# A mixture-of-experts tail that starts one step earlier: first products at step 48, the fourth weight split there, twice the routing from step 45, and the low halves of the second weights last

## The chip, the cores and the metric

The kernel runs on one core of one Trainium2 chip. The time is device microseconds of that core, the median of three runs. The profile is one further execution, with its own time.

## The reference, cut to what matters

Attention over short windows and block sums gives `x` (3072 tokens of 512). Every token then goes to one of 16 experts, chosen in two levels, and the expert's two products give its output row.

```python
g_idx = np.argmax(x @ w_group, axis=1)                   # 4 groups
e_idx = np.argmax(xg @ w_expert[g], axis=1)              # 4 experts in each
h  = np.maximum(xg[mask_e] @ w1[g, e], 0.0)              # 512 -> 1024
ye = h @ w2[g, e]                                        # 1024 -> 512
out[tok_idx] = (g_w * e_w)[mask][:, None] * ye
```

## The kernel before

Every engine has its own queue, and the order in each queue is the order in which the program writes its instructions; nothing is reordered by a scheduler.

**Attention** is a loop over `n` from 0 to 50. Sixteen pairs of heads have three groups of query tiles each, so 48 steps have scores, and steps 48 to 50 only drain the pipeline. A step writes the letters of `PLAN[n % 3]` in order: `s` scores, `e` exponentials, `t` transposes of the probabilities of step n-2, `v` the products with the values of step n-3, `l0` to `l3` the router logits of earlier pairs of heads (`l0` and `l1` transpose parts of `x`, `l2` multiplies them with the router weights, `l3` puts the logits in place), `p` and `b` the preparation of the next pair. At the end of each step `hook(n, ...)` writes a piece of the expert part.

**Routing** of a quarter of the tokens (768) is a generator, `Router.route`, of some thirty small VectorE operations and seven small TensorE products (the ranks). It is drawn forward by `advance(ops)` at places in `scores` and `values` (`OPS`: one operation after the scores, one after the reciprocal, one after the multiplication). The third quarter's routing is put on the list at step 40 behind `first_blocks`, which picks the fullest expert and the tokens of its first four blocks of 128. What is left of the list after the loop is written out at once. The fourth quarter's, with the tables of all later units, is `fin`; it can start only after attention.

**The first expert**, `Experts.first()`, is also a generator. Its weights are kept as two numbers each, a rounded high half (ScalarE copies it, `w1h`, `w2h`) and a low half (VectorE subtracts, `w1l`, `w2l`); so are its inputs (`xT`) and its hidden values (`hTh`, `hTl`). `split_w` makes one of four parts of either weight. `stage1_2` does the first products for 256 tokens in eight portions of 12 TensorE products (128 hidden columns each); here a portion is called a block, 0 to 7. After each second block the ReLU and its low half follow. The results lie in PSUM banks that are used in rotation, so block 6 needs the bank that the low half of blocks 2 and 3 frees. `stage2` does the second products for 128 tokens, 24 in four portions.

Step numbers that matter: `hook(47)` transposes the first 256 tokens (`x_t1`) and splits part 3 of the first weights; `FIRST` says how many portions of `first()` are written in `hook(49)`, `hook(50)` and `hook(51)`, the last of which stands behind the loop: two, one and one.

After attention, `first()` and `fin` are woven by a count of planned time: after each portion, operations of `fin` are drawn while the counted VectorE time is behind the counted TensorE time. Every VectorE operation of the expert part counts, the low halves of weights too. At the tag `units` everything left of `fin` is written, and the weights and tokens of the later experts' units follow.

```python
        for tag in first:
            ...
            while clock.dve < clock.pe and idle < 2:
                before = clock.dve
                next(fin, None)
```

Of the kernel before, what the change touches and what calls it, by code (L numbers as in the profile page):

```python
# [8 lines left out]
F32 = mybir.dt.float32  # L9
# [5 lines left out]
ALU = mybir.AluOpType  # L15
# [5 lines left out]
P = 128  # L21
# [25 lines left out]
KC, FC = DM // P, FF // P  # L47
# [13 lines left out]
OPS = dict(r=1, m=1, k=2, s=(1, 1, 1))  # L61


W1_AT = 34
GATHER_AT, W2_AT, X_AT = 4, 2, 1
SPLIT_AT = (-4, -3, -2, -1)
FIRST = {1: 2, 2: 1, 3: 1}

XT_AT = 4

# [4 lines left out]
class Banks:  # L75
# [5 lines left out]
    def next(self):  # L81
        self.n += 1
        return self.tiles[(self.n - 1) % len(self.tiles)]
# [6 lines left out]
class Clock:  # L90

    pe, dve = float("-inf"), 0.0
    step = 0


def columns(ap):
# [494 lines left out]
def attention(tc, q, k, v, w_group, w_expert, ident, x_dram, ps, router, hook):  # L591
# [3 lines left out]
    clock = router.clock  # L595

    def advance(ops):

        for _ in range(ops):
            r = next(work[0], work) if work else "wait"  # L600
            if r is work:
                work.pop(0)
            elif r == "wait":
                break
# [11 lines left out]
    with ExitStack() as st, ExitStack() as nat_st:  # L616
# [6 lines left out]
        order = [(b, a) for b in range(B) for a in range(NP)]  # L623
# [37 lines left out]
        t = ps_lg.next()  # L661
# [57 lines left out]
        def block_sums(idx):  # L719

            sp = ps_tr.next()[:, 0:2 * D]
            va = va_ring[idx % NVA]
            for i in range(NQT // 4):
                for j in range(4):
                    T.matmul(out=sp[32 * j:32 * j + 32], lhsT=pick[:, i], rhs=va[0:KW, NQT // 4 * j + i, :, 0:D],
                             start=(i == 0), stop=(i == NQT // 4 - 1), skip_group_check=True)
            vss[idx] = sm.tile([P, 2 * D], F32, name="vs", bufs=2)
            V.tensor_copy(out=vss[idx], in_=sp)
# [67 lines left out]
        def scores(n):  # L796

            idx, g = n // 3, n % 3
            qt, kw = qts[idx % 2], kws[idx % 2]
            sp = [ps_s.next()[:, 0:2 * NC].rearrange("p (j c) -> p j c", j=2) for _ in range(2)]  # L800
            for j in range(2):
                for i, h in ((0, 0), (1, 1), (1, 0), (0, 1)):
                    t, rows = 4 * g + 2 * j + i, slice(64 * h, 64 * h + 64)
                    T.matmul(out=sp[h][64 * i:64 * i + 64, j], lhsT=qt[rows, QT * t:QT * t + QT],
                             rhs=kw[rows, t], start=True, stop=True, skip_group_check=True)
            nm = sm.tile([P, 4], F32, name="nm")
            ss = sm.tile([P, 4, NC], F32, name="ss", bufs=2)
            for h in range(2):
                for j in range(2):
                    u, t = 2 * h + j, 4 * g + 2 * j  # L810
                    V.tensor_tensor_reduce(out=ss[:, u], in0=mask[:, 1 if t == 0 else 2 if t == NQT - 2 else 0],  # L811
                                           in1=sp[h][:, j], scale=1.0, scalar=3.4e38, op0=ALU.add, op1=ALU.min,
                                           accum_out=nm[:, u:u + 1])
            advance(OPS["s"][g])
            return ss, nm
# [90 lines left out]
        for n in range(NG + 3):  # L906
            idx, g = n // 3, n % 3
            if n < NG:
                b, a = order[idx]
                xs[b] = x_ring[b % 2]  # L910
            for step in PLAN[g]:
                if step == "s" and n < NG:
                    sps = scores(n)
                    if n == 0:
                        block_sums(0)
                        put_vs(0)
                        router.consts()
                elif step == "e" and n < NG:
                    prs[n] = exps(n, *sps)
                elif step == "t" and 0 <= n - T_LAG < NG:  # L920
                    pts[n - T_LAG] = transpose_p(prs.pop(n - T_LAG))
                elif step == "v" and 0 <= n - V_LAG < NG:
                    values((n - V_LAG) // 3, (n - V_LAG) % 3, pts.pop(n - V_LAG))
                elif step[0] == "p" and n < NG and idx + 1 < len(order):
                    prep(idx + 1, int(step[1]))
                elif step == "b" and n < NG and idx + 1 < len(order):
                    block_sums(idx + 1)
                elif step[0] == "l" and 0 <= idx - LAG[step] < len(order):
                    logits(idx - LAG[step], int(step[1]))
            if n == 0:  # L930
                init_va(2)
                spread_vs(0)
                init_va(3)
            if n in ROUTE_AT:
                b1 = ROUTE_AT.index(n)
                work.append(router.route(b1 * TB, (b1 + 1) * TB))
                if b1 == 1:
                    work.append(router.first_blocks())
            if n == NG - 4:
                nat_st.close()  # L940
            if n < NG:
                if g == 0 and 0 < idx < len(order) - 3:
                    qk[idx + 3] = load_qk(idx + 3)
                if g == 0 and idx + 2 < len(order):
                    load_vw(idx + 2)
                if g == 2 and idx + 1 < len(order):
                    put_vs(idx + 1)
                if g == 0 and idx > 0:
                    spread_vs(idx)
            if g == 1 and stores:  # L950
                store()
            while stores and n == NG - 5:
                store()
            clock.step += 1
            hook(n, need, w1_space)
        for part in (1, 2):
            logits(len(order) - 1, part)
# [9 lines left out]
class Experts:  # L967
# [79 lines left out]
            cs = slice(n * hh, n * hh + n)  # L1047
            queue.dma_start(out=dst[:, cs], in_=src[bass.ds(e, 1), :, cs].rearrange("a p c f -> (a p) c f"), **kw)

    def split_w(self, row, which, parts, copy=None, sub=None):  # L1050

        raw = self.raw(row, which)
        for c in parts:
            js = slice(2 * c, 2 * c + 2)
            if which == 0:
                src = raw.rearrange("p c (j r) -> p c j r", j=FC)[:, :, js]
                h, l = (t[:, :, js] for t in self.w1s)
            else:
                src = raw[:, js]
                h, l = (t[:, js] for t in self.w2s)  # L1060
            (copy or self.nc.scalar.copy)(out=h, in_=src)  # L1061
            (sub or self.V).tensor_tensor(out=l, in0=src, in1=h.bitcast(F32), op=ALU.subtract)

    def gather(self, row, dst, half=0):
        name, c = self.col(row, half)
# [13 lines left out]
        nc.scalar.copy(out=hi, in_=tp)  # L1079
        self.V.tensor_tensor(out=lo, in0=tp, in1=hi.bitcast(F32), op=ALU.subtract)  # L1080

    def stage2(self, hT, row, half=0, b=0):

        nc = self.nc
        yp = self.bank("av", b)
        wh, wl = self.w2s
        hi, lo = hT
        for c in range(FC):
            for i, (a, w) in enumerate(((hi, wh), (hi, wl), (lo, wh))):
                self.T.matmul(out=yp, lhsT=a[:, c], rhs=w[:, c], start=(c == 0 and i == 0),  # L1090
                                 stop=(c == FC - 1 and i == 2), skip_group_check=True)
            if c % 2 == 1:
                yield
        if not self.fixed:
            self.ny = (self.ny + 1) % 2
        y = self.y[b if self.fixed else self.ny]
        name, col = self.col(row, half)
        w = self.tabs[name, "weight"][:, col:col + 1]
        self.nc.scalar.activation(out=y, in_=yp, func=AF.Copy, scale=w)  # L1099
        self.put(y, row, half)  # L1100
# [160 lines left out]
    def first(self):  # L1261
        for i in range(0, NE, 2):
            for k, _ in enumerate(self.stage1_2(0)):
                if i == 0 and k >= 4:
                    self.split_w(("first", 0), 1, [k - 4])
                yield
            if i + 2 < NE:
                self.x_t1()
                yield
            for half in range(2):  # L1270
                s2 = self.stage2([t[:, :, half * P:half * P + P] for t in self.hT2], ("first", i + half))
                if i + half < NE - 1:
                    yield from s2
        yield "units"
        for part, _ in enumerate(s2):
            self.split_w(("unit", 0), 0, [part])
            if part == 0:
                self.x_t2(0)
                for i in range(2):
                    self.gather_one(i)  # L1280
                self.gather_small(0)
        self.fixed = True
# [51 lines left out]
def block_attention_then_moe(tc, q, k, v, w_group, w_expert, w1, w2, out):  # L1334
    with ExitStack() as st:
# [15 lines left out]
        def hook(n, need, space):  # L1351

            if not ex.w1r and n >= W1_AT and (router.ready & 1 or n == last - 4):
                need(1)
# [14 lines left out]
            for part in range(4):  # L1369
                if n == last + SPLIT_AT[part]:  # L1370
                    ex.split_w(("first", 0), 0, [part])
            for _ in range(FIRST.get(n - last, 0)):
                next(first)
# [63 lines left out]
```

## Time and profile before

| | |
|---|---|
| median of three runs | 547.08 us (546.47 to 547.29) |
| time of the profiled execution | 550.22 us |
| its span, first to last instruction | 548.4 us |
| TensorE matmul busy | 495.0 us, 90% |
| VectorE busy | 312.6 us, 57% |
| ScalarE busy | 289.4 us, 53% |
| GpSimd busy | 150.3 us, 27% |
| mean granted TensorE clock | 0.961 |

The busy shares are means over stages. Attention fills about the first 199 us of the span, the first expert's four blocks reach to about 257 us, and units of other experts, with weights loaded meanwhile, fill the rest.

### The profile page before, as it was taken

The page shows a single profiled execution, that of the slowest core. Times are in us where ns is not written, and L with a number is a line of the kernel's source. Part 1 is how long each engine was busy: PE and PEld are TensorE (multiplying, and loading weights), DVE is VectorE, ACT ScalarE, POOL GpSimd, SP SyncE. Part 2 cuts the span into 40 slices and gives each one's busy share as a digit, 9 for nine tenths or more (in the row PEclk, how much of TensorE's full clock was granted, in tenths as well). Part 3 has the DMA queues.
Part 4 walks back from the last instruction along what each step waited for, and adds up shares of the span by engine and source line. Part 5 has one row for each costly group of instructions (what it writes and reads, how often), then busy time and mean ns, then how long its engine had stood idle before and what let it go on. Part 6 is the DMA issues. An engine that isn't in the chain of part 4 may idle for free. (4 is left out here: it accounts for less than half of the span.)

```text
span 548.4 us, 13166 instructions
## 1 busy us (share of the span) xinstructions
PE 495.0 (90%) x4873; PEld 415.3 (76%) x4873; DVE 312.6 (57%) x1001; ACT 289.4 (53%) x561; POOL 150.3 (27%) x166
## 2 busy tenths in 40 slices
PE   6799888898988688999989999899999999999991
PEld 3577666676767577978959788788898998977770
DVE  6667788788876558856725436274564737540000
ACT  5678878899977423114715444364454735541110
POOL 6453453363444100035222040412120212201110
PEclk9789999999988799988998999999999999999997
DMA  9676785695671620099916969666667657746950
GB/s 211 151 179 133 182 194 141 160 219 145 144 272 40 232 77 16 24 331 388 384 51 265 393 222 395 232 237 247 218 231 250 208 179 228 258 118 214 322 195 22
DMA packets 80837, 111.15 MB, mean 203 GB/s; under 512 B 42732, under 2 KB 51310, under 8 KB 77936
## 3 DMA queue, kind: packets, MB, share of 16 engines
q1 hardware_dynamic: 74992, 93.31, 54.8%
q0 software_dynamic: 4704, 14.69, 7.2%
q10 hardware_dynamic: 1056, 2.10, 1.1%
q8 instruction: 44, 0.72, 0.6%
q14 instruction: 41, 0.34, 0.2%
HBM read 118.27 MB, written 13.04 MB: 239 GB/s over the span
## 5 line engine op out<-in xcount | busy, mean ns | idle before, releaser
L122 PE MATMUL ps_s<-xT,w1h 128*128 128x256 f32 x448 | 85.0, 287 | 1.9 <-DVE hTl L122 1.4
L122 DVE TENSOR_TENSOR w2l<-w2r,w2h 128x1024 fp32r<-128x1024 f32 x40 | 48.8, 1225 | 54.3 <-ACT w2h L1061 52.4
L1105 POOL DMA_INDIRECT out_dram<-y,t_unit_scatter x21 | 21.9, 1044 | 196.4 <-ACT y L1099 107.8
L122 PEld LDWEIGHTS ps_s<-xT,w1h 128*128 128x128 f32 x448 | 71.4, 193 | 3.3 <-DVE hTl L122 1.7
L122 PE MATMUL ps_s<-xT,w1l 128*128 128x256 f32 x224 | 63.7, 284 | 0.0
L820 ACT ACTIVATE pr<-ss,nm 128x120 f32<-128x120 f32 x192 | 60.1, 388 | 4.4 <-DVE nm L811 4.0
L1143 ACT ACTIVATE hTh<-ps_s 128x512 fp32r<-128x512 f32 x44 | 26.3, 598 | 53.1 <-PE ps_s L122 33.1
L749 POOL TENSOR_TENSOR va<-vr,share 24x512 f32<-24x512 f32 x48 | 49.7, 1060 | 12.5 <-DMA vr<-vs 8.9
L122 DVE TENSOR_TENSOR w1l<-w1r,w1h 128x1024 fp32r<-128x1024 f32 x40 | 46.4, 1221 | 2.9 <-ACT w1h L1061 2.7
L122 PE MATMUL ps_s<-ohr,w1h 128*128 128x256 f32 x256 | 47.8, 285 | 0.0
L122 DVE SCALAR_TENSOR_TENSOR hTl<-ps_s,hTh 128x512 fp32r<-128x512 f32 x44 | 30.4, 691 | 25.2 <-ACT hTh L1143 24.3
L811 DVE CUSTOM_DVE_ANT_0 ss<-mask,ps_s 128x120 f32<-128x120 f32 x192 | 41.9, 273 | 4.2 <-ACT pr L820 2.4
L1061 ACT CAST w2h<-w2r 128x1024 fp32r<-128x1024 f32 x40 | 41.5, 1042 | 4.3 <-DVE w_all L122 3.6
L122 PEld LDWEIGHTS ps_s<-xT,w1l 128*128 128x128 f32 x224 | 43.2, 193 | 0.2
L122 PEld LDWEIGHTS ps_s<-ohr,w1h 128*128 128x128 f32 x256 | 40.3, 190 | 0.7 <-issue 0.6
L828 ACT COPY ptS<-ps_tr 121x512 f32<-121x512 f32 x48 | 28.2, 587 | 20.9 <-PE ps_tr L122 9.4
L1061 ACT CAST w1h<-w1r 128x1024 fp32r<-128x1024 f32 x40 | 38.9, 1047 | 0.0
L789 POOL COPY kw<-kf 128x1152 f32<-128x1152 f32 x15 | 17.4, 1157 | 77.5 <-DVE kf L780 43.4
L776 ACT ACTIVATE qt<-ps_tr 64x384 f32<-64x384 f32 x64 | 33.3, 521 | 7.2 <-PE ps_tr L122 6.4
L122 PE MATMUL ps_s<-kw,qt 64*64 64x120 f32 x768 | 34.4, 287 | 2.9 <-DVE kw L756 2.1
L122 PE MATMUL ps_av<-va,ptS 121*64 121x65 f32 x768 | 34.3, 234 | 2.8 <-POOL va L749 1.4
L122 PE MATMUL ps_s<-ohr,w1l 128*128 128x256 f32 x128 | 36.2, 283 | 0.0
(255 smaller groups left out, 1055.7 us busy)
## 6 DMA issues: line engine op xcount, KB each, us to landing
w1r<-in_moe_w_dram SPq DMA_DIRECT2D x40, 1024.0 KB
w2r<-in_moe_w_dram SPq DMA_DIRECT2D x40, 1024.0 KB
va<-in_v_dram SPq DMA_DIRECT2D x32, 240.0 KB
kn<-in_k_dram SPq DMA_DIRECT2D x16, 384.0 KB
qn<-in_q_dram SPq DMA_DIRECT2D x16, 384.0 KB
x_dram<-xt SPq DMA_DIRECT2D x12, 512.0 KB
w_first<-in_moe_w_dram SPq DMA_DIRECT2D x2, 1024.0 KB
w2r<-in_moe_w_dram ACTq DMA_DIRECT2D x2, 1024.0 KB
```

Of the source, the lines that this page charges most:

```text
L122: return f(*args, **kw)
L749: nc.gpsimd.tensor_tensor(out=va_ring[idx % NVA][KW:NC, t:t + n, :, 0:D], in0=vr[KW:NC].broadcast_to([NBLK, n, 2, D]), in1=by(share, KW, N ...
L776: nc.scalar.activation(out=by_run(qb, h)[:, j], in_=tv, func=AF.Copy, scale=-1.0 / 8.0)
L789: (nc.gpsimd if idx else V).tensor_copy(out=kw[:, :, 0:KW], in_=tiles)
L811: V.tensor_tensor_reduce(out=ss[:, u], in0=mask[:, 1 if t == 0 else 2 if t == NQT - 2 else 0], in1=sp[h][:, j], scale=1.0, scalar=3.4e38, ...
L820: nc.scalar.activation(out=pr[:, i, 0:NC], in_=sp[:, i], func=AF.Exp, bias=nm[:, i:i + 1], scale=-1.0)
L828: nc.scalar.copy(out=ptS.rearrange("p a c -> p (a c)"), in_=pt[0:NR])
L1061: (copy or self.nc.scalar.copy)(out=h, in_=src)
L1105: self.nc.gpsimd.indirect_dma_start(out=out, out_offset=bass.IndirectOffsetOnAxis(ap=self.tabs[name, "scatter"][:, col:col + 1], axis=0), ...
L1143: nc.scalar.activation(out=th[:, js], in_=hp, func=AF.Relu)
```

## The change

Four things are edited. Part 3 of the first weights is split in `hook(48)` and not in `hook(47)` (`SPLIT_AT`). One portion of `first()` is written in each of `hook(48)` to `hook(51)`, where two, one and one stood in the last three (`FIRST`). From step 46 on, every `advance` draws twice as many routing operations (`MORE_AT`, `MORE`; the step number is noted only at the end of a step, so 45 takes effect in step 46). And the four low halves of the first expert's second weights leave the first products' portions: each is now written in front of a pair of columns of the first `stage2`, in which all products with low halves of weights stand behind the other sixteen.

```diff
+MORE_AT, MORE = 45, 2
-SPLIT_AT = (-4, -3, -2, -1)
-FIRST = {1: 2, 2: 1, 3: 1}
+SPLIT_AT = (-4, -3, -2, 0)
+FIRST = {0: 1, 1: 1, 2: 1, 3: 1}
@@ advance
-        for _ in range(ops):
+        for _ in range(ops * (MORE if clock.n >= MORE_AT else 1)):
@@ attention, end of a step
             clock.step += 1
+            clock.n = n
             hook(n, need, w1_space)
@@ split_w(self, row, which, parts, what="hl")
-            (copy or self.nc.scalar.copy)(out=h, in_=src)
-            (sub or self.V).tensor_tensor(out=l, in0=src, in1=h.bitcast(F32), op=ALU.subtract)
+            if "h" in what:
+                self.nc.scalar.copy(out=h, in_=src)
+            if "l" in what:
+                self.V.tensor_tensor(out=l, in0=src, in1=h.bitcast(F32), op=ALU.subtract)
@@ stage2(self, hT, row, half=0, b=0, late=None)
-        for c in range(FC):
-            for i, (a, w) in enumerate(((hi, wh), (hi, wl), (lo, wh))):
-                self.T.matmul(out=yp, lhsT=a[:, c], rhs=w[:, c], start=(c == 0 and i == 0),
-                                 stop=(c == FC - 1 and i == 2), skip_group_check=True)
-            if c % 2 == 1:
+        terms = (hi, wh), (hi, wl), (lo, wh)
+        if late:
+            order = [(c, t) for c in range(FC) for t in (0, 2)] + [(c, 1) for c in range(FC)]
+        else:
+            order = [(c, t) for c in range(FC) for t in range(3)]
+        for k, (c, t) in enumerate(order):
+            a, w = terms[t]
+            if late and t == 0 and c % 2 == 0:
+                late(c // 2)
+            self.T.matmul(out=yp, lhsT=a[:, c], rhs=w[:, c], start=(k == 0), stop=(k == len(order) - 1),
+                          skip_group_check=True)
+            if k % 6 == 5:
                 yield
@@ first
                 if i == 0 and k >= 4:
-                    self.split_w(("first", 0), 1, [k - 4])
+                    self.split_w(("first", 0), 1, [k - 4], what="h")
...
-                s2 = self.stage2([t[:, :, half * P:half * P + P] for t in self.hT2], ("first", i + half))
+                s2 = self.stage2([t[:, :, half * P:half * P + P] for t in self.hT2], ("first", i + half),
+                                 late=None if i + half else lambda c: self.split_w(("first", 0), 1, [c], what="l"))
```

## Rows read from the trace of the kernel before

**Rows 1.** Windows: length, busy us (instructions) of each engine, clock, DMA share, GB/s.

```profile
160.00:200.00 40.00, 33.52 (x388) 27.34 (x389) 20.04 (x87) 19.44 (x44) 11.35 (x10) 0.83 0.41 146
...
400.00:440.00 40.00, 40.00 (x268) 36.75 (x267) 26.82 (x28) 22.86 (x30) 7.16 (x7) 1.00 0.62 214
```

**Rows 2.** Waits of TensorE, 170 to 262 us: total us, times, longest.

```profile
PE ps_lg L122 <- DVE xT L865: 3.9, 3, 2.5
PE ps_tr L122 <- DVE eb L122: 1.7, 1, 1.7
PE ps_s L122 <- DVE hTl L122: 1.4, 1, 1.4
PE ps_av L122 <- DVE mx L122: 1.3, 1, 1.3
```

**Rows 3.** Windows of 4 us around step 48, columns as in rows 1.

```profile
184.00:188.00 4.00, 1.25 (x11) 0.42 (x11) 2.99 (x8) 1.38 (x2) 0.00 (x0) 0.66 0.84 322
188.00:192.00 4.00, 4.00 (x32) 3.64 (x29) 0.84 (x4) 0.59 (x1) 0.00 (x0) 0.50 0.29 108
192.00:196.00 4.00, 4.00 (x45) 3.76 (x44) 0.68 (x4) 1.28 (x3) 0.00 (x0) 0.98 0.33 126
```

**Rows 4.** Timeline of TensorE, steps 48 to the first second products: start, us, instruction.

```profile
183.23 0.69 PE L122 MATMUL ps_av<-va,ptS 121*64 121x65 f32 x16 [1.31 <-DVE mx L122]
...
187.18 0.87 PE L122 MATMUL ps_lg<-xT,wcat 128*32 128x192 f32 x8 [2.50 <-DVE xT L865]
...
190.19 0.58 PE L122 MATMUL ps_s<-xT,w1h 128*128 128x256 f32 x1
...
194.01 0.60 PE L122 MATMUL ps_tr<-ident,xt 128*128 128x128 f32 x4
...
195.16 0.38 PE L122 MATMUL ps_s<-xT,w1h 128*128 128x256 f32 x1
...
199.67 0.22 PE L122 MATMUL ps_tr<-eb,tri 128*128 128x96 bf16 x1
...
204.47 0.39 PE L122 MATMUL ps_s<-xT,w1h 128*128 128x256 f32 x1 [1.45 <-DVE hTl L122]
...
207.45 1.13 PE L122 MATMUL ps_tr<-ident,xg 128*128 128x128 f32 x8
208.34 0.47 PE L122 MATMUL ps_av<-w2h,hTh 128*128 128x512 f32 x1
```

**Rows 5.** Timeline of TensorE, the rest of the first pair's second products.

```profile
214.42 0.20 PE L122 MATMUL ps_tr<-eb,tri 128*128 128x96 bf16 x1 [1.65 <-DVE eb L122]
...
216.17 0.48 PE L122 MATMUL ps_s<-w2h,hTh 128*128 128x512 f32 x1
...
221.83 0.28 PE L122 MATMUL ps_s<-xT,w1h 128*128 128x256 f32 x1
```

**Rows 6.** Timeline of VectorE, step 47 to the fourth quarter's routing.

```profile
183.50 1.29 DVE L122 TENSOR_TENSOR xT<-ps_tr,xT 128x512 fp32r<-128x512 f32 x2 [0.22 <-ACT xT L1079]
184.92 1.23 DVE L122 TENSOR_TENSOR w1l<-w_first,w1h 128x1024 fp32r<-128x1024 f32 x1
...
186.71 0.42 DVE L865 COPY xT<-ps_tr 128x256 f32<-128x256 f32 x1
...
205.13 2.36 DVE L122 TENSOR_TENSOR w2l<-w2r,w2h 128x1024 fp32r<-128x1024 f32 x2 [0.71 <-ACT w2h L1061]
...
212.07 0.27 DVE L122 TENSOR_REDUCE mx<-lg 128x30 f32<-128x120 f32 x1
```

**Rows 7.** Timeline of ScalarE, the first high halves of second weights.

```profile
204.05 2.00 ACT L1061 CAST w2h<-w2r 128x1024 fp32r<-128x1024 f32 x2 [3.58 <-DVE w_all L122]
```

**Rows 8.** The page's groups: busy us, mean ns of one, idle before.

```profile
L1143 ACT ACTIVATE hTh<-ps_s 128x512 fp32r<-128x512 f32 x44 | 26.3, 598 | 53.1 <-PE ps_s L122 33.1
L122 DVE SCALAR_TENSOR_TENSOR hTl<-ps_s,hTh 128x512 fp32r<-128x512 f32 x44 | 30.4, 691 | 25.2 <-ACT hTh L1143 24.3
```

**Rows 9.** Timeline of the SP queue: the first loads of a unit's weights.

```profile
233.47 0.92 SPq L1048 DMA_DIRECT2D w1r<-in_moe_w_dram  x2
```

More of the change, by code (lines that the diff above doesn't have):

```diff
@@ L92 @@
     pe, dve = float("-inf"), 0.0
-    step = 0
+    step, n = 0, 0
 def columns(ap):
@@ L1048, in load_w, with split_w @@
             queue.dma_start(out=dst[:, cs], in_=src[bass.ds(e, 1), :, cs].rearrange("a p c f -> (a p) c f"), **kw)
-    def split_w(self, row, which, parts, copy=None, sub=None):
+    def split_w(self, row, which, parts, what="hl"):
         raw = self.raw(row, which)
@@ L1080, in split_t, with stage2 @@
         self.V.tensor_tensor(out=lo, in0=tp, in1=hi.bitcast(F32), op=ALU.subtract)
-    def stage2(self, hT, row, half=0, b=0):
+    def stage2(self, hT, row, half=0, b=0, late=None):
         nc = self.nc
```

## The prediction

> **What bounds the kernel now.** I read the windows first. In a later stage TensorE is busy for all of 40 us at full clock; from 160 to 200 us it is busy for 33.5 of 40 at a granted clock of 0.83, with VectorE at 20.0 and ScalarE at 19.4 [rows 1]. So TensorE sets the pace, and the turn from attention to the first expert is where it loses time, without another engine being full. The list of TensorE's waits says by whom: all the large ones end at VectorE [rows 2]. The timeline then places them: 1.31 us at 183.23 before the values of step 45, 2.50 at 187.18 before the logits `l2` of step 49, 1.45 at 204.47 before block 6 [rows 4], and 1.65 at 214.42 before the fourth quarter's rank products [rows 5]. [...] The two blocks that start at 190.19 need 3.82 us to 194.01, where the two from 204.47 to 207.45 need 2.98 [rows 4]. The change touches all but the first of these.
>
> **Step 47 to block 3.** VectorE's queue explains the 2.50 us. The low halves of `xT` run from 183.50 for 1.29, then the low half of weight part 3 from 184.92 for 1.23, and only behind it the copy at 186.71 (0.42) that `l2` waits for [rows 6]. With part 3 a step later that copy moves up by about a microsecond, and block 0 stands in TensorE's queue ahead of `l2`, so the wait is filled twice over. The split itself is moved, not removed: its subtraction now follows the copy, and nothing needs it before block 6; if that cover were gone it would cost its 1.23.
>
> Up to 183.23 I expect no change. The routing drawn in steps 46 and 47 is about ten operations instead of five. By the 0.27 of one such operation [rows 6] that is at most 1.35 us more on VectorE, spread over two steps in which the values wait 1.31 anyway [rows 4]; I take 0. In step 48 the doubled routing already writes the third quarter's rank products, and these take a transpose bank in the rotation of three. So `l1`'s transposes must now wait for the second low half of `xT`, to 183.50 + 1.29 = 184.79, and block 0 starts at about 185.2 (0.4 for two transposes; four start and yield to the next work within the 1.15 from 194.01 to 195.16 [rows 4]).
>
> Block 0 costs 1.49 at full clock (half of 2.98) and at most 2.98 at the lower level. The window around it showed 0.66, and TensorE has just had gaps, so I put it at the lower level, where the measured pair allows at least 3.82 - 1.49 = 2.33; I take 2.6, to 187.8. `l2`, the transposes and the values of step 49 took 3.01 (187.18 to 190.19) at the lower level; at full clock I estimate 1.5. With gaps gone the clock should rise in between: 2.0, to 189.8. Block 1 takes 1.49 (191.3). The next 1.15 (194.01 to 195.16) stays (192.45). From there to 199.67 it was 4.51 [rows 4]; I add 0.4, because about four routing operations (0.27 each) now stand on VectorE in front of the copy that the last `l2` waits for, and that wait was already part of the 3.9 [rows 2]. Block 3 ends at 197.4 instead of 199.67: **2.3 us gained**. Bounds: full clock throughout gives 185.2 + 1.49 + 1.5 + 1.49 + 1.15 + 4.9 = 195.8, a gain of 3.9; the lower level until 192, as before, leaves about 0.5.
>
> [...]
>
> **The rest of routing and block 6.** Before, the rest of the third quarter's routing is written behind block 3 and VectorE works on it up to 204 us. It keeps the low half of hidden values back, on whose bank block 6 waits 1.45 [rows 4], and it keeps ScalarE's first `w2h` back by 3.58 [rows 7]. After, twenty-two of the twenty-seven operations are written inside the loop, and five are left, some 1.35 us at 0.27. ReLU and low half take 0.60 + 0.69 = 1.3 [rows 8], while block 6 comes two blocks, 2.98, later, so it finds its bank free. The third quarter's rank products leave this stretch, the fourth quarter's take their place (by the planned clock `fin` is first drawn after block 4, now that no low half of a weight is counted there). **1.5 us gained**; bounds 1.0 and 1.7.
>
> **The low halves last.** Before, from 207.45 to the second half's products at 216.17 it is 8.72 us, of which 1.65 is the wait for the routing [rows 4, 5]: VectorE starts the fourth quarter only at 212.07, behind the four `w2l` (2.36 for two) [rows 6]. After, that routing has been done among blocks 4 to 7, and the wait is gone. In its place comes one for the low halves. Counted from the end of block 7: ReLU and low half to 1.3, the two low halves of `xT` (1.29) to 2.6, then a `w2l` each 1.18: 3.8, 4.95, 6.1, 7.3. TensorE transposes for 0.89 (207.45 to 208.34), and its sixteen products without a low weight take 16/24 of 5.66 (216.17 to 221.83) [rows 4, 5], to 4.7. The first two parts are there; the third makes it wait 0.5, the fourth 0.7. It ends at 7.3 + 0.47 = 7.8 instead of 8.72: **0.9 us gained**. Bounds: no wait at all, 0.89 + 5.66 = 6.55, gives 2.2; low halves that start only when TensorE asks for them (4.7 + 4 x 1.18 + 0.47 = 9.9) cost 1.2.
>
> **Behind that** I expect a plain shift. `fin` is drawn against TensorE's planned time, so the second pair's products keep their place beside it, and the first loads of unit weights at 233.47 [rows 9] leave earlier with it. I take 0, from -0.5 to 0.5.
>
> **Sum:** 2.3 + 1.5 + 0.9 = 4.7 us. The profiled execution (span 548.4, time 550.22) would take 545.5. It lies 3.1 above the median of the runs, so I apply the difference there: 547.08 - 4.7 = 542.4.
>
> **Rivals.** *The clock stays up*: 3.9 + 1.5 + 0.9 = 6.3, so 540.8. [...] Against: the gap of 1.31 and the wait for the bank remain in front of block 0. *The clock stays down until 192*: 0.5 + 1.5 + 0.9 = 2.9, 544.2. For it: the rows of 184 to 192; against: the 2.50 gap that lay in them is gone. *Nothing is passed on*: the units' weights or the routing tables, not TensorE, decide when the units begin, and TensorE waits there for what it saved; 547.1. Against it, the fourth quarter's routing also begins more than ten microseconds earlier than 212.07 (behind block 4, at about 199). *Slower*: routing gets in front of the low halves on VectorE, at the first `stage2`. What was issued from 212.07 to 221.83 is 9.8 us; all of it ahead of `w2l` would give 4.7 - 9.8 = -5.1, so 552.2, and from 4.7 us on it decides. Against it, the planned clock counts `w2l` and draws no routing while VectorE is ahead. That the change does not act at all is excluded by the order of the queues.
>
> **How the numbers follow.** Forecast 0.48, clock up 0.25, clock down 0.14, nothing passed on 0.08, slower 0.05. The forecast's own range is 541.3 to 543.5. From 539.8 (clock up, with up to a microsecond more from fewer waits for low halves) to 545.2 (clock down, with a microsecond more of waits) it holds the first three but for their tails. A measurement here tells 0.2% (1.1 us) from no change: faster by more than that 0.87, within it 0.08, slower 0.05.
>
> **What would show it.** Right: block 0 starts near 185 and `l2` follows it without a gap; block 6 without a wait; a wait of about a microsecond for `w2l` late in the first second products; rank products of the fourth quarter between blocks 6 and 7; unit weights issued near 228.8. Wrong: a granted clock of 0.50 beyond 190, routing between the four `w2l`, a `w2h` kept back by something other than routing, or new waits of TensorE between 230 and 257 that give the shift back.

## The result, and the profile after

The changed kernel takes 543.06 us (four runs, 542.91 to 543.24) where the kernel before takes 547.18 (546.47 to 547.9): by the medians 4.1 us faster. The ratio of the two kernels on record is 0.9897 (95% interval 0.9863 to 0.9931), which is 5.6 us (3.8 to 7.5); it is not the quotient of these medians, 0.9925, which lies inside the interval. The forecast was 542.4, 4.7 us faster. A second set of runs, told below, gives 0.9885 (0.9851 to 0.9919) and 6.1 us in the medians.

Two places are followed through all runs. The **first stretch** is from the low halves of `xT` in step 47 (VectorE) to the last `l2` of attention (TensorE). The **second stretch** is from that `l2` to the first product of the second pair of token blocks. Before, they are 183.50 to 197.68, 14.18 us, and 197.68 to 221.83, 24.15 us [rows 5, 6]; the 197.68 is this row of the timeline of TensorE before:

```profile
197.68 0.53 PE L122 MATMUL ps_lg<-xT,wcat 128*32 128x192 f32 x8 [0.61 <-DVE xT L865]
```

TensorE's timeline after, the lines that answer to rows 4 and 5 (all line numbers are one higher):

```profile
183.67 0.20 PE L123 MATMUL ps_tr<-eb,tri 128*128 128x96 bf16 x1
...
184.27 0.44 PE L123 MATMUL ps_tr<-ident,xt 128*128 128x128 f32 x2 [0.23 <-DVE xT L123]
184.46 0.36 PE L123 MATMUL ps_s<-xT,w1h 128*128 128x256 f32 x1
...
186.07 0.53 PE L123 MATMUL ps_lg<-xT,wcat 128*32 128x192 f32 x8
...
187.77 0.39 PE L123 MATMUL ps_s<-xT,w1h 128*128 128x256 f32 x1
...
189.30 0.60 PE L123 MATMUL ps_tr<-ident,xt 128*128 128x128 f32 x4
...
193.35 0.53 PE L123 MATMUL ps_lg<-xT,wcat 128*32 128x192 f32 x8 [0.98 <-DVE xT L866]
...
199.67 0.22 PE L123 MATMUL ps_tr<-eb,tri 128*128 128x96 bf16 x1
...
201.46 1.20 PE L123 MATMUL ps_tr<-ident,xg 128*128 128x128 f32 x8
...
206.22 1.10 PE L123 MATMUL ps_av<-w2l,hTh 128*128 128x512 f32 x4
207.59 0.73 PE L123 MATMUL ps_av<-w2l,hTh 128*128 128x512 f32 x2 [0.28 <-DVE w2l L123]
208.73 0.72 PE L123 MATMUL ps_av<-w2l,hTh 128*128 128x512 f32 x2 [0.40 <-DVE w2l L123]
209.29 0.40 PE L123 MATMUL ps_s<-w2h,hTh 128*128 128x512 f32 x1
...
214.89 0.28 PE L123 MATMUL ps_s<-xT,w1h 128*128 128x256 f32 x1
```

The reader sees the order that was forecast. The third quarter's rank products stand in step 48, `l1` waits 0.23 us for the second low half of `xT`, block 0 lies between `l1` and `l2`, and `l2` at 186.07 has no wait where it had 2.50 [rows 4]. The last `l2` waits 0.98, where it waited 0.61 (the line above). Blocks 4 to 7 follow each other with the fourth quarter's rank products (199.67) in between and no wait for a bank, where block 6 waited 1.45 [rows 4]. The products with low halves stand last and wait 0.28 and 0.40.

VectorE after, with `w2l` in one run of four behind the low halves of `xT`, as forecast:

```profile
182.92 1.29 DVE L123 TENSOR_TENSOR xT<-ps_tr,xT 128x512 fp32r<-128x512 f32 x2
...
185.59 0.42 DVE L866 COPY xT<-ps_tr 128x256 f32<-128x256 f32 x1
185.93 1.22 DVE L123 TENSOR_TENSOR w1l<-w_first,w1h 128x1024 fp32r<-128x1024 f32 x1
...
204.05 4.62 DVE L123 TENSOR_TENSOR w2l<-w2r,w2h 128x1024 fp32r<-128x1024 f32 x4
```

Windows of 4 us after, to set beside rows 3:

```profile
184.00:188.00 4.00, 3.77 (x47) 3.10 (x45) 2.97 (x11) 1.39 (x2) 0.00 (x0) 1.00 0.97 370
188.00:192.00 4.00, 4.00 (x45) 3.76 (x45) 2.21 (x12) 1.09 (x2) 0.00 (x0) 1.00 0.39 146
```

TensorE is busy for 3.77 of 4 us where it was for 1.25, and the granted clock is 1.00 where it was 0.66 and 0.50. The 0.50 of rows 3 is what the prediction and the expectations call the lower level, and 1.00 is their full clock. The first stretch is 193.35 - 182.92 = 10.43 us (3.75 less), the second 214.89 - 193.35 = 21.54 (2.61 less). The first loads of unit weights answer to rows 9:

```profile
226.46 0.94 SPq L1050 DMA_DIRECT2D w1r<-in_moe_w_dram  x2
```

They leave 7.0 us earlier, and the profiled executions differ by as much: 550.22 against 543.24. The 7.0 is not the worth of the change: the profiled execution of before was a long one, and the control's, 544.22, has these loads at 232.29, 5.8 us behind the change's.

### The profile page after: what moved, and what is told of

It is laid out like the page before. It is cut to its first block, busy times and chain, and to the rows that moved or that the text cites. A ratio compares the mean times of both kernels' runs of the same rounds, so it can differ in the third digit from the quotient of the medians.

```text
span 541.5 us, 13168 instructions
## 1 busy us (share of the span) xinstructions
PE 492.9 (91%) x4873; PEld 412.7 (76%) x4873; DVE 312.2 (58%) x1001; ACT 289.0 (53%) x561; POOL 151.2 (28%) x166
## 5 line engine op out<-in xcount | busy, mean ns | idle before, releaser
L123 DVE SCALAR_TENSOR_TENSOR hTl<-ps_s,hTh 128x512 fp32r<-128x512 f32 x44 | 30.4, 690 | 27.7 <-ACT hTh L1154 27.7
L123 PE MATMUL ps_s<-w2h,hTh 128*128 128x512 f32 x88 | 35.7, 406 | 0.0
```

What stands on the lines that cost most here:

```text
L123: return f(*args, **kw)
```

## The experiments

All ratios are times against the kernel before, on the same chip in the same set; below 1 is faster. The start and end points of the two stretches are rows of each run's own timelines.

| run | xT low halves | last `l2` | second pair | first stretch | second stretch | ratio (95%) |
|---|---|---|---|---|---|---|
| before | 183.50 | 197.68 | 221.83 | 14.18 | 24.15 | |
| before again (e_ctl) | 182.96 | 196.50 | 220.66 | 13.54 | 24.16 | 1.0003 (0.9981 to 1.0026) |
| e_split | 182.67 | 196.07 | 220.23 | 13.40 | 24.16 | 0.9962 (0.9939 to 0.9984) |
| e_first | 182.65 | 193.96 | 218.13 | 11.31 | 24.17 | 0.9917 (0.9884 to 0.9949) |
| e_start | 182.21 | 193.35 | 217.50 | 11.14 | 24.15 | 0.9932 (0.9902 to 0.9962) |
| e_more | 181.24 | 195.67 | 216.15 | 14.43 | 20.48 | 0.9937 (0.9910 to 0.9964) |
| e_low | 185.61 | 200.54 | 224.79 | 14.93 | 24.25 | 1.0009 (0.9986 to 1.0031) |
| the change | 182.92 | 193.35 | 214.89 | 10.43 | 21.54 | 0.9897 (0.9863 to 0.9931) |
| the change again (a_again) | 182.67 | 193.10 | 214.62 | 10.43 | 21.52 | 0.9885 (0.9851 to 0.9919) |
| x_low | 185.62 | 196.82 | 217.31 | 11.20 | 20.49 | 0.9885 (0.9848 to 0.9921) |
| i_early | 181.41 | 191.83 | 212.24 | 10.42 | 20.41 | 0.9871 (0.9837 to 0.9905) |
| i_act | 182.89 | 192.78 | 213.27 | 9.89 | 20.49 | 0.9851 (0.9809 to 0.9892) |
| i_best | 182.23 | 192.15 | 212.55 | 9.92 | 20.40 | 0.9858 (0.9822 to 0.9893) |

The second stretch repeats within 0.1 us for kernels that are alike in it; the first varies by up to 1.4 between executions that are alike in it (13.54 in e_ctl, 14.93 in e_low), whose granted clocks differ: in the three windows of 4 us from 184 on they are 1.00, 0.57 and 1.00 in e_ctl and 0.72, 0.50 and 0.50 in e_low. So effects under a microsecond are read from the stretches, and the ratios tell the larger ones.

**Each part alone.** The start alone (e_start):

```diff
-SPLIT_AT = (-4, -3, -2, -1)
-FIRST = {1: 2, 2: 1, 3: 1}
+SPLIT_AT = (-4, -3, -2, 0)
+FIRST = {0: 1, 1: 1, 2: 1, 3: 1}
```

> Only the first part of the change: part 3 of the first weights split at step 48, one portion in each of steps 48 to 51; routing and low halves as before. Theory 1, three separate gains that add up (start, routing, low halves): the 2.5 us wait before l2 of step 49 goes, the waits of 1.45 and 1.65 us stay; 1.6 us faster if the measured 4.1 us less 1.6 and 0.9 for the other two is what is left for it, up to 3.9 if it is what the two profiles show. Theory 2, the granted clock: the profile of before was an execution with a low clock at 184 to 192 us, which its other executions need not have; then this run gains less than 1 us in the median, and its profile shows full clock there.

Measured: 544.89 against 548.93 us. The first stretch is 11.14, the second unchanged at 24.15. TensorE's waits between 168 and 262 us are those of before without the 2.50:

```profile
PE ps_tr L122 <- DVE eb L122: 1.6, 1, 1.6
PE ps_s L122 <- DVE hTl L122: 1.5, 1, 1.5
PE ps_lg L122 <- DVE xT L865: 1.4, 2, 0.8
```

The granted clock fell here too, to 0.58 in the window 184 to 188, and the start gained all the same:

```profile
184.00:188.00 4.00, 4.00 (x37) 3.05 (x35) 1.61 (x4) 0.47 (x2) 0.00 (x0) 0.58 0.80 306
188.00:192.00 4.00, 4.00 (x50) 3.70 (x46) 1.86 (x8) 1.49 (x4) 0.00 (x0) 1.00 0.36 135
```

The first rows of block 0, `l2` and block 1 in that run:

```profile
183.15 0.37 PE L122 MATMUL ps_s<-xT,w1h 128*128 128x256 f32 x1
...
185.71 0.87 PE L122 MATMUL ps_lg<-xT,wcat 128*32 128x192 f32 x8
...
188.14 0.39 PE L122 MATMUL ps_s<-xT,w1h 128*128 128x256 f32 x1
```

The control, told below, has one of the two windows at a low clock too (0.57), and against it the stretch is 2.40 us shorter, where the wait was 2.50. So theory 2, that the start's gain is the clock's, does not hold; the gain is the filled wait.

The routing alone (e_more):

```diff
+MORE_AT, MORE = 45, 2
-        for _ in range(ops):
+        for _ in range(ops * (MORE if clock.n >= MORE_AT else 1)):
+            clock.n = n
```

> Only the doubled routing from step 46. Theory 1, three separate gains: the 1.45 us wait of block 6 goes, the 1.65 us wait for the fourth quarter's routing stays; 1.5 us faster. Theory 3, the routing's rest is the cause of both later waits: with it gone VectorE and ScalarE start on the second weights some 3 us earlier, so VectorE also comes to the fourth quarter in time, and both waits go; 3.0 us faster, with no wait over 0.3 us between blocks 6 and 7 and the second half's products.

Measured: 545.28 against 548.93 us, and 3.67 us off the second stretch, of which the two waits were 3.10. The first stretch is no shorter (14.43). That is theory 3: both later waits go, though low halves of weights stand where they stood before. In the list of TensorE's waits (168 to 262 us) neither `eb` nor `hTl` is left, and the fourth quarter's rank products have no wait behind eighteen second products:

```profile
PE ps_lg L123 <- DVE xT L866: 3.8, 3, 2.4
PE ps_lg L123 <- DVE few L123: 0.9, 1, 0.9
PE ps_s L123 <- DVE nm L812: 0.6, 1, 0.6
```

```profile
208.74 0.20 PE L123 MATMUL ps_tr<-eb,tri 128*128 128x96 bf16 x1
```

VectorE starts the fourth quarter's routing at 206.39, 10.72 us behind the last `l2`, where it was 212.07 - 197.68 = 14.39 before:

```profile
206.39 0.27 DVE L123 TENSOR_REDUCE mx<-lg 128x30 f32<-128x120 f32 x1
```

The low halves alone (e_low; `split_w`, `stage2` and `first` as in the change, the constants as before):

```diff
-                    self.split_w(("first", 0), 1, [k - 4])
+                    self.split_w(("first", 0), 1, [k - 4], what="h")
...
+                                 late=None if i + half else lambda c: self.split_w(("first", 0), 1, [c], what="l"))
```

> Only the low halves last. Theory 1: the 1.65 us wait goes and about 0.7 comes in its place, 0.9 us faster. Theory 3: the rest of the third quarter's routing still holds VectorE up to the end, the 1.45 us wait of block 6 stays, the fourth quarter's rank products now wait about 0.4 us between blocks 6 and 7, and the low halves 0.7 us; 0.3 us faster, not to be told from no change.

Measured: 549.18 against 548.93 us, no change, and none in the second stretch (24.25 against 24.15). Three waits stand in it where two stood: for the bank as before, for ScalarE's `hTh` ahead of the rank products, and for low halves:

```profile
PE ps_s L123 <- DVE hTl L123: 1.5, 1, 1.5
...
PE ps_av L123 <- DVE w2l L123: 0.7, 2, 0.4
...
PE ps_tr L123 <- ACT hTh L1154: 0.6, 1, 0.6
```

Theory 3 put the wait at the rank products at 0.4 and on VectorE; it is 0.56 and the profile names ScalarE, though VectorE's `eb` is ready only at 209.51, 0.10 before the products start. VectorE begins the fourth quarter 207.21 - 200.54 = 6.67 us behind the last `l2`, earlier than in e_more:

```profile
207.21 0.27 DVE L123 TENSOR_REDUCE mx<-lg 128x30 f32<-128x120 f32 x1
209.31 0.20 DVE L123 CAST eb<-eoh 128x96 bf16<-128x96 f32 x1
```

**The change without its low halves last** (x_low):

```diff
-                    self.split_w(("first", 0), 1, [k - 4], what="h")
+                    self.split_w(("first", 0), 1, [k - 4])
...
-                                 late=None if i + half else lambda c: self.split_w(("first", 0), 1, [c], what="l"))
+                                 late=None)
```

> The change without its last part: low halves of the second weights in the first products' portions, as before. Theory 1: 0.9 us slower than the whole change, 3.2 us faster than before. Theory 3: VectorE has done all four low halves by about 1 us after block 7 and comes to the fourth quarter's routing about when TensorE needs it, so the 1.65 us wait is gone without the move, and the 0.7 us wait for low halves that the move brings is gone too; about 1.2 us faster than the whole change, 5.3 us faster than before.

Measured: 543.04 against 548.93 us, and a second stretch of 20.49, 1.05 shorter than the change's. The ratio cannot tell it from the change. VectorE finishes the fourth quarter's `eb` just as TensorE asks for it:

```profile
203.47 2.36 DVE L123 TENSOR_TENSOR w2l<-w2r,w2h 128x1024 fp32r<-128x1024 f32 x2
...
209.65 0.20 DVE L123 CAST eb<-eoh 128x96 bf16<-128x96 f32 x1
```

```profile
209.90 0.20 PE L123 MATMUL ps_tr<-eb,tri 128*128 128x96 bf16 x1
```

So by the second stretch the low halves last cost about a microsecond once the routing is early. The first stretch is 11.20, with a wait of 0.71 ahead of `l2` of step 49 that the change does not have and whose cause is open, so the two stretches together are 31.7 us against the change's 32.0, where 1.2 us less was expected.

**The start in two halves.** e_split takes only `SPLIT_AT = (-4, -3, -2, 0)`, e_first only `FIRST = {0: 1, 1: 1, 2: 1, 3: 1}`.

> Of the start only its first half: part 3 of the first weights split at step 48, portions as before (two, one, one in steps 49 to 51). Theory 1 (the wait before l2 of step 49 is filled twice over): the copy that l2 waits for moves up by the subtraction's 1.2 us, the wait falls from 2.5 to about 1.3, 1.2 us faster. Theory 2 (the granted clock is what the start gains): TensorE still has gaps among transposes, the clock stays at the lower level between 184 and 192 us, less than 1 us faster.

> Of the start only its second half: one portion in each of steps 48 to 51, part 3 split at step 47 as before. Theory 1: block 0 lies in the wait before l2 and costs nothing; the wait falls below 0.8 us, 1.5 to 2.5 us faster, and with both halves of the start not much more. Theory 2: the block also keeps the clock up in 184 to 192 us; 3 us and more faster, with a granted clock over 0.9 in both windows.

Measured: 544.52 and 542.69 against 546.42 us. The row of `l2` in step 49, of e_split and then of e_first:

```profile
184.99 0.87 PE L122 MATMUL ps_lg<-xT,wcat 128*32 128x192 f32 x8 [1.14 <-DVE xT L865]
```

```profile
186.34 0.87 PE L122 MATMUL ps_lg<-xT,wcat 128*32 128x192 f32 x8 [0.24 <-DVE xT L865]
```

Moving the subtraction leaves 1.14 of the 2.50, block 0 in front of `l2` leaves 0.24. They work on one wait, as theory 1 has it. Against the two executions of before the first stretch is 0.1 to 0.8 us shorter in e_split and 2.2 to 2.9 in e_first; both halves together give 2.4 to 3.0. In e_split less is gained than the 1.36 us of wait that went, and the clock is low in both windows (0.55 and 0.59), as theory 2 said for this run:

```profile
184.00:188.00 4.00, 3.01 (x29) 2.06 (x29) 2.06 (x6) 1.13 (x2) 0.00 (x0) 0.55 0.91 345
188.00:192.00 4.00, 4.00 (x23) 4.00 (x22) 0.84 (x4) 0.00 (x0) 0.00 (x0) 0.59 0.37 139
```

In e_first too the clock is 0.57 in 184 to 188, so the block did not keep it up. The median of e_first is 3.7 us lower, more than its stretch gives and than the 1.5 to 2.5 of theory 1; where the rest lies is not shown.

**Two additions.** i_early is the change with the first low half written behind block 6; i_act is x_low with the copies of the last two pairs' `l1` on ScalarE:

```diff
+                if i == 0 and k == 6:
+                    self.split_w(("first", 0), 1, [0], what="l")
...
-                                 late=None if i + half else lambda c: self.split_w(("first", 0), 1, [c], what="l"))
+                                 late=None if i + half else lambda c: c and self.split_w(("first", 0), 1, [c], what="l"))
```

```diff
-                (V.tensor_copy if part else nc.scalar.copy)(
+                (V.tensor_copy if part and idx < len(order) - 2 else nc.scalar.copy)(
```

> The whole change with the first of the four low halves written behind block 6, where VectorE stood idle 1.3 us. If the two waits of 0.3 and 0.4 us for low halves come from the length of VectorE's chain behind block 7, they go: 0.7 us from the last l2 of attention to the second pair's first product (20.8 instead of 21.5 us). If the products with low halves are held up by something else, they stay. In the times 0.7 us can hardly be told.

> The change without low halves last, and with the copies of the transposed logits' input of the last two pairs of heads made by ScalarE, which is idle there, and not by VectorE behind the routing. If VectorE's queue is what the last two l2 wait for (0.7 and 1.0 us), the waits fall to about 0.2 and 0.5, 0.5 to 1.0 us faster than without that edit. If ScalarE's other work gets in the way (the cast of part 3, the probabilities' copies), no change.

Measured: i_early has no wait for low halves left, and its second stretch is 20.41; 0.4 more than expected is gained. Its rank products of the fourth quarter stand behind block 7 and not behind block 6; whether the 0.4 comes from that is not shown. i_act's last `l2` waits for ScalarE, and less:

```profile
192.78 0.53 PE L123 MATMUL ps_lg<-xT,wcat 128*32 128x192 f32 x8 [0.46 <-ACT xT L866]
```

Its first stretch is 9.89, 0.54 below the change's. Both kernels (539.7 and 538.95 against 546.42 us) are faster than before beyond doubt; that they are faster than the change is told by the stretches.

**Control, the change again, and both additions.** e_ctl is the kernel before, a_again the change, i_best the change with both additions.

> The kernel before, run against itself: what this measurement tells from no change, and a second profile of it. Expected ratio 1.000 within 0.3%. Theory 2 (the granted clock) takes the first profile's low clock behind step 48 for an accident; then this profile shows the stretch from step 48's l1 to the last l2 well under 13.4 us, at 11 or less. If the low clock there belongs to the kernel, it is 13 to 14 us again, and from the last l2 to the second pair's first product 24.15 us.

> The change again, beside the next kernel: ratio 0.990 within 0.3%; 9.1 us from step 48's l1 to the last l2 (up to 10.4 where the clock falls there) and 21.5 us from the last l2 to the second pair's first product.

> The change with both additions: one of the four low halves written behind block 6, and the last two pairs' copies on ScalarE. If the two are separate, 8.5 us from step 48's l1 to the last l2 and 20.4 from there to the second pair's first product, 1.6 us less than the change together; ratio 0.985 to 0.987, 1.6 us below the change. If one takes the other's cover (ScalarE late for the second weights' high halves), the second stretch is over 21.

Measured: 545.69, 539.86 and 537.84 against 545.98 us. The control shows no difference from itself within 0.3%. Its second profile keeps the 2.50 wait and all of the second stretch, and its clock is 1.00 in 184 to 188 and 0.57 in 188 to 192:

```profile
184.00:188.00 4.00, 1.50 (x22) 0.93 (x22) 2.45 (x7) 0.99 (x3) 0.61 (x1) 1.00 0.90 325
188.00:192.00 4.00, 4.00 (x34) 3.93 (x29) 0.84 (x4) 0.43 (x1) 0.00 (x0) 0.57 0.48 182
```

From step 48's `l1` to the last `l2` it is 196.50 - 183.70 = 12.80 us, a little under the 13 to 14 that was expected if the low clock belongs to the kernel, and far from the 11 if it does not. So both executions of the kernel before have a low clock here, 0.66 and 0.50 in the two windows of the first [rows 3], 1.00 and 0.57 in those of the second, and its place moves by some microseconds between them. The change repeats as expected: 9.09 from `l1` to the last `l2`, 21.52 behind it. i_best has 30.3 us in the two stretches together against 32.0 for the change and 38.3 for before, which is the 1.6 us that was expected of it. But i_act, without the low halves last, has 30.4, and the ratio does not tell the two apart either: the last part of the change is not needed for the best of these times.

## Why the prediction was right

The time came near the forecast (4.1 and, again, 6.1 us less in the medians, for 4.7). Two of its three gains came from what it named, and that the number came so near is in part luck. The two stretches together lost 6.4 us, or 5.7 from the control's, nearer to the 6.3 of the rival "the clock stays up" than to 4.7, and the ratio of the first set (5.6 us, 3.8 to 7.5) holds both. By its steps:

- **Step 47 to block 3**, forecast 2.3, bounds 0.5 and 3.9. The first stretch lost 3.75 us, or 3.1 from the control's. The filled wait, the delayed `l1` and the longer wait of the last `l2` (0.4 more, as charged) came as written. What was mis-sized is the clock: block 0 was put at the lower level, with 2.6 us, and the work between it and block 1 at 2.0. In the change they take 186.07 - 184.46 = 1.61 and 187.77 - 186.07 = 1.70, at a granted clock of 1.00 both times the change ran; in e_start, at 0.58 in 184 to 188, they take 185.71 - 183.15 = 2.56 and 188.14 - 185.71 = 2.43, and its first stretch is 11.14. The rival "the clock stays up" had the case for the change; a low clock is what the start alone met. That the clock falls with TensorE's gaps and rises when they are gone was the author's estimate from rows 3, and the runs do not show it as a rule: in e_start TensorE is busy for all of 184 to 188 at 0.58, and in the change for 2.79 of the 4 us from 180 to 184 at 1.00. Why the clock was 1.00 in 184 to 188 in the change and 0.58 in e_start, without the doubled routing, is open: with the doubled routing alone (e_more) it is 0.90 there and 0.67 in 188 to 192, and in x_low, which has both, 0.80 and 1.00. In the change it had fallen earlier, to 0.50 in 172 to 176 us; in i_best it was 1.00 from 172 to 192 throughout.
- **The rest of routing and block 6**, forecast 1.5. From the last `l2` to the transposes ahead of the second products it is 201.46 - 193.35 = 8.11 us, where it was 207.45 - 197.68 = 9.77: 1.66 gained.
- **The low halves last**, forecast 0.9. From the transposes to the second half's products it is 209.29 - 201.46 = 7.83, where it was 8.72 [rows 4, 5]: 0.89 gained, with waits of 0.28 and 0.40 where 0.5 and 0.7 were worked out. The number is right by luck, and the credit is wrong. The step says that the fourth quarter's routing is reached in time because low halves no longer stand in front of it. The routing alone does that (e_more, 3.67 us off the second stretch for 1.5 + 0.9 forecast), and moving the low halves gives 1.05 of it back. Before, VectorE came late to the fourth quarter for two reasons: the rest of the third quarter's routing, which also kept ScalarE's high halves back [rows 7], and the low halves' own 4.7 us. It began 14.39 us behind the last `l2`; the early routing alone makes that 10.72, the moved low halves alone 6.67. The wait was only 1.65, so either edit is about enough for it. But the early routing also ends the wait for the bank, and moving the low halves leaves that wait and adds others (e_low). The step did not ask what its own routing step had already done for this wait. A forecast part by part, and not of the sum, would have been wrong here: about 3.6 for the routing, none or a loss for the low halves.
- **Behind that**, forecast a plain shift. From the second pair to the last scatter the change takes 530.88 - 214.89 = 315.99 and, again, 526.97 - 214.62 = 312.35 us:

```profile
530.88 0.99 POOL L1116 DMA_INDIRECT out_dram<-y,t_unit_scatter  x1 [12.12 <-ACTq L1307]
```

```profile
526.97 1.00 POOL L1116 DMA_INDIRECT out_dram<-y,t_unit_scatter  x1 [12.12 <-ACTq L1307]
```

The kernel before takes 316.03 and, in the control, 311.29 for the same (its rows stand below). It varies by 4.7 us in one kernel, so no profile can show that nothing at all was given back. What speaks for a plain shift are the times: 6.1 us in the medians of the second set and ratios of 5.6 and 6.3 us, beside 5.7 to 6.4 in the stretches. The rivals "nothing is passed on" and "slower" did not come.

- **The profile as a measure.** The forecast applied its sum to the median and took the profiled execution for a typical one. The control's profile is 544.22 us, 6.0 less than the first. From the second pair to the units' first product it is 34.12 where the first has 35.72 (221.83 to 257.55). From there to the last scatter (its row and the first profile's, below, with the unit's first product) it is 277.2 against 280.3.

```profile
254.78 0.28 PE L122 MATMUL ps_s<-xT,w1h 128*128 128x256 f32 x1
...
531.95 0.99 POOL L1105 DMA_INDIRECT out_dram<-y,t_unit_scatter  x1 [12.13 <-ACTq L1295]
```

```profile
257.55 0.28 PE L122 MATMUL ps_s<-xT,w1h 128*128 128x256 f32 x1
...
537.86 1.00 POOL L1105 DMA_INDIRECT out_dram<-y,t_unit_scatter  x1 [12.12 <-ACTq L1295]
```

Neither of these two lies in the stretches that the change works on; both are of the kernel before.

## What to carry to other kernels

Before crediting a wait to the work that stands directly in front of it, ask what made that work late: here one leftover of routing lay behind two waits (1.45 and 1.65 us [rows 4, 5]) and held a third engine (3.58 [rows 7]), and the edit at the last of them was worth nothing by itself. A long, ready piece of work put in front of a waiting instruction on the same engine filled the wait at a granted clock of 0.58 (e_start) and of 1.00 (the change); moving the late producer up took 1.36 of 2.50 off the wait, about the 1.23 [rows 6] of the subtraction that had stood in front of it, and the stretch kept at most 0.8 of it (e_split). Measure a part alone and the whole without it: the sum of several parts can be right while one of them costs time.

## What the hardware showed that was not expected

One VectorE operation that runs beside GpSimd's products ended with them, and took the longer the earlier it started. In step 46 the subtraction `dd` (128x120) takes 1.02 us in the change, where the same operation for the fourth quarter takes 0.28 at 197.09, with GpSimd idle from 196 to 200. It ends at 177.97, 0.14 behind GpSimd's three products from 173.81 (173.81 + 4.02 = 177.83). In the kernel before it starts later beside the same products, takes 0.73, and ends at 178.55, again 0.14 behind them (174.39 + 4.02 = 178.41). In e_more it ends 0.14 behind them (175.24 + 1.02 against 172.10 + 4.02), in x_low 0.13 (179.64 + 1.02 against 176.50 + 4.03). The change's rows, VectorE and GpSimd, and then those of before:

```profile
176.95 1.02 DVE L123 TENSOR_TENSOR dd<-lg,mx 128x120 f32<-128x120 f32 x1
...
197.09 0.28 DVE L123 TENSOR_TENSOR dd<-lg,mx 128x120 f32<-128x120 f32 x1
```

```profile
173.81 4.02 POOL L750 TENSOR_TENSOR va<-vr,share 24x512 f32<-24x512 f32 x3 [2.58 <-issue]
```

```profile
177.82 0.73 DVE L122 TENSOR_TENSOR dd<-lg,mx 128x120 f32<-128x120 f32 x1
```

```profile
174.39 4.02 POOL L749 TENSOR_TENSOR va<-vr,share 24x512 f32<-24x512 f32 x3 [2.56 <-issue]
```

Why they end together is not shown. The scaling of attention's values (`xt`) stands behind `dd` on VectorE, and the transposes of `l0` wait 0.29 us for that (1.30 in x_low). Whether this costs anything is not shown; the values of step 45 wait anyway, 1.09 after for 1.31 before [rows 4].
